# Six tiles of normalised rows transposed on VectorE, GpSimd and ScalarE instead of TensorE, and one product of the last network moved ahead of another

## The chip, the cores and the metric

The kernel runs on one core of one Trainium2 chip. The metric is the device time of one execution in microseconds (us). Three executions of the kernel before took 541.15, 541.38 and 541.42 us, the median being 541.38. A further execution was profiled; all rows below are from that one.

## The reference

Three stages follow each other. Attention with a local window and block summaries gives rows `x`; a network of eight experts with one expert per row gives new rows `x`; the last stage mixes them by a two-dimensional Fourier transform, normalises each row, and runs a dense network with 2048 hidden units. The change lies in the last stage only:

```python
def _moe2_ref(x, w_ch1, w_ch2):
    X = np.fft.fft(x, axis=1)
    X = np.fft.fft(X, axis=2)
    mixed = np.real(X).astype(np.float32)
    u = x + mixed
    mu = np.mean(u, axis=-1, keepdims=True)
    var = np.mean((u - mu) ** 2, axis=-1, keepdims=True)
    un = (u - mu) / np.sqrt(var + 1e-06)
    ch = np.maximum(un @ w_ch1, 0.0) @ w_ch2
    return (u + ch).astype(np.float32)
```

`x` has 2 x 768 rows of 512 numbers.

## The kernel before

The 1536 rows are twelve tiles of 128 rows, tile 0 to tile 11, and three chunks of four tiles: chunk 0 is tiles 0 to 3, chunk 1 tiles 4 to 7, chunk 2 tiles 8 to 11. The network's matmuls need a chunk's normalised rows with the 512 features on the partitions, so each tile is transposed. Every number is kept as a sum of a high and a low part (`h` and `l`, `fp32r`), and a product is three matmuls: high by high, high by low, low by high.

For one tile the steps are these. `ln_apply(i)` (L800 to L806) writes the normalised rows into a buffer `un` on ScalarE. `ln_T(i)` (L807 to L812) transposes its four 128x128 blocks on TensorE into a PSUM tile `lpt` (L810), ScalarE copies that into the high part `unh` of the chunk and VectorE writes the difference into the low part `unl` (L812). The buffers `un` come from a pool of four.

The network runs over 16 blocks of 128 hidden units, f = 0 to 15. `L1(c,f)` is 12 matmuls of 512 columns for chunk c into a PSUM tile `fph`; then `relu` writes the hidden units' high part `fhh` on ScalarE (L964) and their low part `fhl` on VectorE (L965). `L2(c,f)` is 12 matmuls from these into four PSUM tiles `fpy` (L985). `second()` issues the `L2` of the block before, so the order on TensorE is L1(f), L2(f-1), L1(f+1), L2(f), and so on. Chunk 0 runs all 16 blocks in the first loop (L1001). In it, beside the blocks f = 12 to 15, tiles 4 to 8 are normalised and tiles 4 to 7 transposed. Then comes a loop of eight blocks (L1073), numbered n = 0 to 7: L1(1,0) to L1(1,3) and L1(2,0) to L1(2,3). Beside n = 0 and n = 1 the tiles 8 to 11 are transposed. L1(1,0) reads all of chunk 1, that is tiles 4 to 7; L1(2,0) reads chunk 2.

The other 24 blocks of chunks 1 and 2 run in pairs (`pair`, L1047) by Strassen's scheme: seven half-size products `prod`, each 6 matmuls (L1052), are combined on VectorE into the first layer's results for two blocks and two chunks. `tt` (L1023) is VectorE's or GpSimd's addition. Three `ph` buffers in PSUM take the products in turn. The first pair has a part `begin` (L1093) in which VectorE and ScalarE still prepare factors of the products, `XT[0]` among them.

All engines execute in the order in which the code records their instructions; nothing reorders them. An engine that waits at one instruction holds back all that is recorded behind it.

Of the kernel before, what the change touches and what calls it, by code (L numbers as in the profile page):

```python
# [11 lines left out]
F32=mybir.dt.float32; R=mybir.dt.float32r; BF=mybir.dt.bfloat16; FH=mybir.dt.float16; I32=mybir.dt.int32; U8=mybir.dt.uint8  # L12
# [747 lines left out]
def fft_ffn(tc,ctx,fctx,tctx,cctx,plctx,I,ident,x2_dram,out,W,P,raw):  # L760
# [37 lines left out]
    def un_chunk(c,pool):  # L798
        UN[c]=tuple(pool.tile([128,4,512],R,name=f"un{x}{c}",tag=f"un{x}") for x in "hl")
    LP={}; TP=[None,None]  # L800
    def ln_apply(i,eng=None):
        un=LP.get(i) or unA.tile([128,512],F32,name=f"un{i}",tag="un",bufs=4)
        if i>3: S.activation(un,utile(i),AF.Identity,bias=nt[:,i:i+1],scale=rstd[:,i:i+1])
        elif eng is None: S.activation(un,utile(i),AF.Identity,bias=nb[:,i:i+1])
        else: eng.tensor_scalar(out=un,in0=utile(i),scalar1=nb[:,i:i+1],scalar2=None,op0=ALU.add)
        LP[i]=un  # L806
    def ln_T(i):  # L807
        un=LP.pop(i); c,q=divmod(i,4)
        pt=TP[0].tile([128,4,128],F32,name=f"lpt{i}",tag=TP[1])
# [152 lines left out]
    def hid(c,f): return [hp.tile([128,512],R,name=f"fh{n}{c}_{f}",tag="h"+n) for n in "hl"]  # L962
    def relu(h,x,o=slice(0,512)):
        S.activation(h[0][:,o],x,AF.Relu)  # L964
        V.scalar_tensor_tensor(out=h[1][:,o],in0=x,scalar=0.0,in1=h[0][:,o].bitcast(F32),op0=ALU.max,op1=ALU.subtract)  # L965
    def L1(c,f):
        g,k=divmod(f,4); h,l=W[g,0]; uh,ul=UN[c]
        ph=php.tile([128,512],F32,name=f"fph{c}_{f}",tag="ph"); n=0
        o=slice(128*k,128*k+128)
        for kd in range(4):  # L970
            for a,x in ((h,uh),(h,ul),(l,uh)):
                T.matmul(ph,lhsT=a[:,kd,o],rhs=x[:,kd],start=n==0,stop=n==11); n+=1  # L972
        H[c,f]=hid(c,f); relu(H[c,f],ph)
    def L2(c,f):
        g,k=divmod(f,4); wh,wl=W[g,1]; hh,hl=H.pop((c,f))
        if (c,f) in OPEN: PY[c]=[pyp.tile([128,512],F32,name=f"fpy{c}_{f}_{t}",tag=f"py{t}") for t in range(4)]
        for t in range(4):
            q=slice(128*t,128*t+128)
            if t==3 and c==2 and f>13:
                if f==15: PY[c][3]=(PY[c][3][:,0:256],ptp.tile([128,512],F32,name="fpy2_15_4",tag="pt")[:,0:256])  # L980
                outs=[(y,slice(256*n,256*n+256)) for n,y in enumerate(PY[c][3])]
            else: outs=[(PY[c][t],slice(0,512))]
            for y,o in outs:
                for i,(a,b) in enumerate(((hh,wh),(hh,wl),(hl,wh))):
                    T.matmul(y,lhsT=a[:,q],rhs=b[:,k,o],start=(c,f) in OPEN and i==0,stop=(c,f) in DONE and i==2)  # L985
                if (c,f)==(2,14): store(t,y,o)
    def fin(c,last,ts=range(4)):
        for t in ts:
            i=4*c+t; b,a,w=order[i]; u=utile(i)
            if c: tt(V,u,PY[c][t],u,ADD)  # L990
            else: V.scalar_tensor_tensor(out=u,in0=PY[c][t],scalar=rstd[:,i:i+1],in1=u,op0=ALU.mult,op1=ALU.add)
            o=b*768+w*384+a*128
            if last: nc.sync.dma_start(out[o:o+128],u)
# [3 lines left out]
    def second():  # L997
        if pend:
            c,f=pend.pop(0); L2(c,f)
            if (c,f) in DONE: fin(c,c==0)  # L1000
    for f in range(16):  # L1001
        if f==12: ln_apply(4)
        L1(0,f)
        for _ in range(1 if f in (2,4,7,10,12) else 2):
            if cv.busy: cv.step(); cv.load()
        if f<12: ln_stats((f+4)%12)
        if f==8: ln_rstd(slice(4,12))
        if f==12: ln_rstd(slice(0,4))
        if f==12:
            while cv.busy: cv.step(); cv.load()  # L1010
            rctx.close(); unB=ctx.enter_context(tc.tile_pool(name="unB",bufs=1)); un_chunk(1,unB)
        if f in (13,14): ln_T(2*f-22)
        if f in (13,14): ln_apply(2*f-21)
        if f==15: ln_apply(8)
        second(); pend.append((0,f))
        if f in (13,14):
            ln_T(2*f-21)
            if f==13: ln_apply(6)

    late=ctx.enter_context(tc.tile_pool(name="post",bufs=1)).tile([128,2,512],F32,name="post")  # L1020
# [23 lines left out]
    def pair(g,q,begin,ahead):  # L1044
        f=4*g+2*q; w=W[g,0]; n=[0]
        A=lambda i,j: [[a[:,2*j+k,256*q+128*i:256*q+128*i+128] for k in range(2)] for a in w]
        As=lambda s: [[a[:,s,256*q+128*k:256*q+128*k+128] for k in range(2)] for a in W[g-1,0]]  # L1047
        B=lambda j,k: [[a[:,2*j+i] for i in range(2)] for a in UN[k+1]]
        def prod(l,m):
            ps=php.tile([128,512],F32,name=f"fw{f}_{n[0]}",tag="ph"); n[0]+=1; i=0  # L1050
            for k in range(2):
                for a,b in ((0,0),(0,1),(1,0)): T.matmul(ps,lhsT=l[a][k],rhs=m[b][k],start=i==0,stop=i==5); i+=1  # L1052
            return ps
        def hidden(c,i,x): H[c,f+i]=hid(c,f+i); relu(H[c,f+i],x)
        S.copy(c12,prod(A(0,0),B(0,0))); tt(V,c11,prod(A(0,1),B(1,0)),c12,ADD)
        if begin: begin()
        split=ahead()
        tt(V,c12,prod(As(1),XT[1]),c12,ADD); hidden(1,0,c11)
        tt(V,c21,prod(As(2),XT[2]),c12,ADD)
        p=prod(As(0),XT[0]); tt(V,c22,p,c21,ADD); tt(V,c12,p,c12,ADD)  # L1060
        if begin: fin(2,False)
        tt(V,c21,prod(A(1,1),XT[3]),c21,ADD); hidden(1,1,c21)
        tt(V,c12,prod(As(3),B(1,1)),c12,ADD)
        if not begin: split()
        L2(1,f); hidden(2,1,c22); L2(1,f+1); fin(1,f==14); hidden(2,0,c12)
        if begin: split()
        L2(2,f+1); L2(2,f)
        if f<14: fin(2,False)
# [2 lines left out]
    D=[two(x) for x in xs]; pt=lambda: ptp.tile([128,512],F32,name="stage",tag="pt")  # L1071
    
    for n,(c,f) in enumerate([(1,0),(1,1),(1,2),(1,3),(2,0),(2,1),(2,2),(2,3)]):  # L1073
        if n==0: ln_apply(9)
        if n==2:
            t4=four(D+[None],X4,V,False); BG+=[x for y in t4[0:3] for x in y]
            un4=[unA.tile([128,512],R,name=f"xt{i}",tag="un",bufs=4) for i in range(4)]
            def last(k):
                p=pt(); h,l=X4(1,0); tt(V,p,h[:,k],D[1][:,k],SUB); tt(V,p,p,l[:,k],ADD); parts(un4[k],un4[2+k],p)
            BG+=[lambda k=k: last(k) for k in range(2)]  # L1080
            XT[3]=[un4[0:2],un4[2:4]]
        if n==6:
            sp=[pt()]; sp=[sp[0][:,256*(s%2):256*(s%2)+256] for s in range(4)]; z=weights(1,0,sp,V)
            for s in range(4): BG+=z[s]+[lambda s=s: parts(*place(1,0,s),sp[s])]
        if n==7:
            XT[1]=[[w[:,k] for k in range(2)] for w in W[0,1]]; parts(*[w[:,0:2] for w in W[0,1]],D[1])
        bg((0,0,3,3,2,2,4,6)[n])
        L1(c,f)
        if n<2: ln_T(8+2*n)
        if n==0: ln_apply(10); ln_apply(11)  # L1090
        second(); pend.append((c,f))
        if n<2: ln_T(9+2*n)
    def begin():  # L1093
        XT[2]=[[x[:,k] for k in range(2)] for x in UN[2]]; parts(*[x[:,0:2] for x in UN[2]],D[2])
        bg(4)
        c,f=pend.pop(0); L2(c,f)
        XT[0]=[[w[:,2+k] for k in range(2)] for w in W[0,1]]; parts(*[w[:,2:4] for w in W[0,1]],D[0])
        bg(99)
# [71 lines left out]
```

## Time and profile before

| | |
|---|---|
| median of 3 runs | 541.38 us |
| profiled execution | 541.06 us, of which span 539.2 us |
| TensorE matmuls busy | 526.5 us, 98% of the span |
| VectorE busy | 382.7 us, 71% |
| ScalarE busy | 276.6 us, 51% |
| GpSimd busy | 117.1 us, 22% |

The span runs from the first to the last instruction of the profile; the 1.9 us around it belong to the execution. PE is TensorE's matmuls, PEld its weight loads, DVE is VectorE, ACT ScalarE, POOL GpSimd. A name after L is a line of the kernel before. The modelled end of a matmul overlaps the next one, so the distance of two starts, not the duration, is what a matmul costs TensorE.

### The profile page before, as it was taken

How to read it: one execution, taken by the hardware profiler on the slowest of the kernel's cores; microseconds unless marked ns; L12 is line 12 of the kernel's file. 1: busy time of each engine (PE TensorE's matmuls, PEld its weight loads, DVE VectorE, ACT ScalarE, POOL GpSimd, SP SyncE). 2: the span in 40 equal slices, each digit the busy share in tenths (PEclk: the TensorE clock that was granted, in tenths of full speed). 3: DMA queues.
4: the chain of work that ended last, by engine and by line, in shares of the span. 5: the costliest groups of instructions: out<-in, count | busy, mean ns of one | idle time of the engine just before them, and what ended most of it. 6: DMA issues, size and time to landing. Idle time of an engine off the chain costs nothing.

```text
span 539.2 us, 9090 instructions
## 1 busy us (share of the span) xinstructions
PE 526.5 (98%) x3434; PEld 435.8 (81%) x3435; DVE 382.7 (71%) x731; ACT 276.6 (51%) x547; POOL 117.1 (22%) x163
## 2 busy tenths in 40 slices
PE   8999999999999999999999999999999999999996
PEld 4777778899999998887788888888887788888885
DVE  5778748797878887576887777516866866665664
ACT  5777775465776777543568987533023221221210
POOL 3225260302243202020540000000004345416000
PEclk9999999999999999999999999999999999999999
DMA  8999464698889886133045554002000000000004
GB/s 288 407 365 396 143 215 176 204 331 303 324 313 390 291 325 231 38 121 136 3 156 157 168 157 145 1 0 79 0 1 0 1 0 2 0 1 0 1 0 156
DMA packets 22735, 81.24 MB, mean 151 GB/s; under 512 B 2816, under 2 KB 4735, under 8 KB 19105
## 3 DMA queue, kind: packets, MB, share of 16 engines
q1 hardware_dynamic: 19249, 70.02, 36.6%
q0 software_dynamic: 3296, 10.48, 5.6%
q8 instruction: 28, 0.46, 0.3%
q14 instruction: 18, 0.15, 0.1%
q10 hardware_dynamic: 144, 0.13, 0.1%
HBM read 70.40 MB, written 9.96 MB: 149 GB/s over the span
## 4 chain that ended last, share of the span: by engine, by line
PE 53%; issue 3%; DVE 1%; ACT 0%; POOL 0%; DVEq 0%; POOLq 0%
PE fpy L985 24%; PE fph L972 12%; PE fw L1052 10%; PE py L582 1%; PE s1q L853 1%; PE lpt L810 1%; PE ph L565 1%; PE s L853 1%; PE pp L853 1%; PE big L582 1%; PE pq L853 1%; DVE dwr L1023 0%; DVE fwl L1023 0%; ACT fwh L1034 0%; PE s L867 0%
## 5 line engine op out<-in xcount | busy, mean ns | idle before, releaser
L985 PE MATMUL fpy<-fwh,fhh 128*128 128x512 f32 (+1 forms) x194 | 75.9, 391 | 0.0
L985 PE MATMUL fpy<-fwh,fhl 128*128 128x512 f32 (+1 forms) x194 | 75.5, 389 | 0.0
L985 PE MATMUL fpy<-fwl,fhh 128*128 128x512 f32 (+1 forms) x194 | 75.3, 388 | 0.0
L565 PE MATMUL ph<-xx,wh 128*128 128x256 f32 (+1 forms) x352 | 69.6, 290 | 1.6 <-DVEq L659 1.2
L552 DVE TENSOR_TENSOR wl<-wr,wh 128x1024 fp32r<-128x1024 f32 x46 | 54.6, 1222 | 13.6 <-ACT wh L551 13.5
L565 PEld LDWEIGHTS ph<-xx,wh 128*128 128x128 f32 x352 | 56.0, 191 | 3.7 <-ACTq L659 1.6
L551 ACT CAST wh<-wr 128x1024 fp32r<-128x1024 f32 (+1 forms) x50 | 48.3, 1014 | 12.6 <-PE py L582 7.1
L565 PE MATMUL ph<-xx,wl 128*128 128x256 f32 (+1 forms) x192 | 54.6, 292 | 0.0
L1023 POOL TENSOR_TENSOR dwr<-fwh 128x256 f32<-128x256 f32 x10 | 7.9, 788 | 173.5 <-DVE unl L1023 135.0
L1023 DVE TENSOR_TENSOR dwr<-fpy,dwr 128x512 f32<-128x512 f32 (+1 forms) x57 | 36.2, 676 | 10.5 <-PE fpy L985 10.5
L985 PEld LDWEIGHTS fpy<-fwh,fhl 128*128 128x128 f32 x194 | 36.4, 188 | 8.2 <-DVE fhl L965 0.4
L985 PEld LDWEIGHTS fpy<-fwh,fhh 128*128 128x128 f32 x194 | 36.5, 188 | 7.9 <-ACT fhh L964 0.4
L985 PEld LDWEIGHTS fpy<-fwl,fhh 128*128 128x128 f32 x194 | 36.5, 188 | 7.6
L972 PE MATMUL fph<-unh,fwh 128*128 128x512 f32 x96 | 38.1, 397 | 0.0
L972 PE MATMUL fph<-unh,fwl 128*128 128x512 f32 x96 | 37.7, 393 | 0.0
L972 PE MATMUL fph<-unl,fwh 128*128 128x512 f32 x96 | 37.7, 392 | 0.0
L582 PE MATMUL py<-wh,hh 128*128 128x512 f32 x92 | 36.8, 400 | 0.0
L565 PEld LDWEIGHTS ph<-xx,wl 128*128 128x128 f32 x192 | 36.1, 190 | 0.0
L582 PE MATMUL py<-wl,hh 128*128 128x512 f32 x92 | 36.1, 392 | 0.0
L582 PE MATMUL py<-wh,hl 128*128 128x512 f32 x92 | 36.0, 392 | 0.0
L589 POOL DMA_INDIRECT x_dram<-y,sidx x13 | 14.5, 1117 | 80.4 <-ACT y L587 48.0
L733 DVE SCALAR_TENSOR_TENSOR ft<-ft,fr 128x512 int32<-128x512 int32 x32 | 22.1, 691 | 12.6 <-ACT ft L732 12.5
(373 smaller groups left out, 1175.5 us busy)
## 6 DMA issues: line engine op xcount, KB each, us to landing
wr<-in_wm SPq DMA_DIRECT2D x24, 1024.0 KB, 7.6
fr<-in_wc SPq DMA_DIRECT2D x32, 512.0 KB, 3.6
kw<-in_kw SPq DMA_DIRECT2D x6, 720.0 KB, 11.1
vw<-in_vw SPq DMA_DIRECT2D x4, 1040.0 KB, 8.7
ft<-in_ft POOLq DMA_DIRECT2D x8, 436.0 KB, 9.5
x_dram<-xt SPq DMA_DIRECT2D x12, 256.0 KB, 5.5
dwr<-x_dram SPq DMA_DIRECT2D x12, 256.0 KB, 4.9
out<-dwr SPq DMA_DIRECT2D x11, 256.0 KB, 2.2
```

Of the source, the lines that this page charges most:

```text
L551: if 'h' in what: S.copy(wh[:,o],raw[:,o])
L552: if 'l' in what: eng.tensor_tensor(out=wl[:,o],in0=raw[:,o],in1=wh[:,o].bitcast(F32),op=ALU.subtract)
L565: T.matmul(ph,lhsT=a[:,o],rhs=b[:,kd],start=n==0,stop=n==11); n+=1
L582: T.matmul(PY[s][tt],lhsT=a[:,q],rhs=b[:,o],start=(c==0 and fb==0 and i==0),stop=(c==3 and fb==1 and i==2))
L589: st=G.indirect_dma_start(out=x2_dram[0:1152] if s==LAST else x2_dram,out_offset=IndirectOffsetOnAxis(ap=col,axis=0),in_=y,in_offset=None)
L733: V.scalar_tensor_tensor(out=ti,in0=ti,scalar=3,in1=low,op0=ALU.logical_shift_left,op1=ALU.bitwise_or)
L810: for kd in range(4): T.transpose(pt[:,kd],un[:,kd*128:kd*128+128],ident)
L853: T.matmul(ps,lhsT=ls[l],rhs=rs[r],start=first and n==0,stop=last and n==2); n+=1
L972: T.matmul(ph,lhsT=a[:,kd,o],rhs=x[:,kd],start=n==0,stop=n==11); n+=1
L985: T.matmul(y,lhsT=a[:,q],rhs=b[:,k,o],start=(c,f) in OPEN and i==0,stop=(c,f) in DONE and i==2)
L1023: def tt(e,o,x,y,op): e.tensor_tensor(out=o,in0=x,in1=y,op=op)
L1052: for a,b in ((0,0),(0,1),(1,0)): T.matmul(ps,lhsT=l[a][k],rhs=m[b][k],start=i==0,stop=i==5); i+=1
```

## The change

For tiles 4 to 9, `ln_T` is replaced by two new functions. `ln_S` has VectorE transpose each 32x32 block of the 128x512 tile within its place, from `un` into a buffer `tb`; 16 copies of 32 partitions x 4 x 32 numbers then move the blocks to their places in a buffer `xt_`, 10 of them on GpSimd (`G`) and 6 on ScalarE (`S`). `ln_P` then splits `xt_` into `unh` and `unl`; its operands lie in SBUF where those of L812 lay in PSUM. `un`, `tb` and `xt_` share the pool of four buffers. Tiles 10 and 11 keep `ln_T`. A table `plan`, read by `ln_at`, says before or after which block each step is recorded. It has ten entries, of which two stand below; A is `ln_apply`, B `ln_S`, C `ln_P`.

In the pair with `begin`, the product of `A(1,1)` and `XT[3]` is recorded before that of `As(0)` and `XT[0]`. Its use on VectorE stays in its place.

```diff
+    XS={}
+    def ln_S(i):
+        un=LP.pop(i)
+        b=unA.tile([128,512],F32,name=f"tb{i}",tag="un",bufs=4); XS[i]=unA.tile([128,512],F32,name=f"xt_{i}",tag="un",bufs=4).rearrange("p (k t) -> p k t",k=4)
+        V.transpose(b,un); b=b.rearrange("p (k j t) -> p k j t",k=4,j=4)
+        for q in range(4):
+            for j in range(4): (S.copy if (4*q+j)%8 in (2,5,7) else G.tensor_copy)(XS[i][32*j:32*j+32,:,32*q:32*q+32],b[32*q:32*q+32,:,j])
+    def ln_P(i):
+        x=XS.pop(i); c,q=divmod(i,4); o=slice(128*q,128*q+128); h,l=UN[c]
+        S.copy(h[:,:,o],x); V.tensor_tensor(out=l[:,:,o],in0=x,in1=h[:,:,o].bitcast(F32),op=ALU.subtract)
...
+    A,B,C=ln_apply,ln_S,ln_P
+    plan={(12,0):((A,4),),(12,1):((B,4),(A,5),(B,5)),(13,1):((C,4),(A,6),(B,6)),(13,2):((C,5),(A,7)),(14,1):((B,7),(C,6),(A,8)),
...
+    def ln_at(f,i):
+        for x,y in plan.get((f,i),()): x(y)
...
-        if f in (13,14): ln_T(2*f-22)
-        if f in (13,14): ln_apply(2*f-21)
-        if f==15: ln_apply(8)
+        ln_at(f,1)
...
         tt(V,c21,prod(As(2),XT[2]),c12,ADD)
+        if begin: p3=prod(A(1,1),XT[3])
         p=prod(As(0),XT[0]); tt(V,c22,p,c21,ADD); tt(V,c12,p,c12,ADD)
         if begin: fin(2,False)
-        tt(V,c21,prod(A(1,1),XT[3]),c21,ADD); hidden(1,1,c21)
+        tt(V,c21,p3 if begin else prod(A(1,1),XT[3]),c21,ADD); hidden(1,1,c21)
```

On ScalarE, from the last square root of the statistics to the activation of L1(0,14), the order before is this; `fph0_13` is L1's result for chunk 0 and block 13, and `lpt4` tile 4 transposed by TensorE:

```order
L783 ACTIVATE rstd_3493<-var_3492,eps_3498 128x4
L964 ACTIVATE fhh0_13_4650<-fph0_13_4637 128x512
L812 CAST unh1_4623<-lpt4_4654 128x4x128
L803 ACTIVATE un5_4661<-dwr1_3259,nt_3494,rstd_3493 128x512
L812 CAST unh1_4623<-lpt5_4675 128x4x128
L803 ACTIVATE un6_4682<-dwr1_3259,nt_3494,rstd_3493 128x512
L964 ACTIVATE fhh0_14_4697<-fph0_14_4684 128x512
```

The same stretch of ScalarE now, with `tb4` tile 4 transposed by blocks and `xt_4` tile 4 put together:

```order
L783 ACTIVATE rstd_3493<-var_3492,eps_3498 128x4
L819 COPY xt_4_4626<-tb4_4625 32x4x32 x6
L803 ACTIVATE un5_4644<-dwr1_3259,nt_3494,rstd_3493 128x512
L819 COPY xt_5_4647<-tb5_4646 32x4x32 x6
L974 ACTIVATE fhh0_13_4690<-fph0_13_4677 128x512
L822 CAST unh1_4623<-xt_4_4626 128x4x128
L803 ACTIVATE un6_4696<-dwr1_3259,nt_3494,rstd_3493 128x512
L819 COPY xt_6_4699<-tb6_4698 32x4x32 x6
L822 CAST unh1_4623<-xt_5_4647 128x4x128
L803 ACTIVATE un7_4731<-dwr1_3259,nt_3494,rstd_3493 128x512
L974 ACTIVATE fhh0_14_4746<-fph0_14_4733 128x512
```

Twelve copies and one `un` now stand ahead of the activation of block 13, and six more copies with two casts and two `un` ahead of that of block 14.

On VectorE, behind the last step of the statistics, the order before is this (`fhl0_13` is the low part of block 13's hidden units):

```order
L789 TENSOR_TENSOR nt_3494<-nb_3495,rstd_3493 128x4
L965 SCALAR_TENSOR_TENSOR fhl0_13_4651<-fph0_13_4637,fhh0_13_4650 128x512
L812 TENSOR_TENSOR unl1_4624<-lpt4_4654,unh1_4623 128x4x128
L812 TENSOR_TENSOR unl1_4624<-lpt5_4675,unh1_4623 128x4x128
L965 SCALAR_TENSOR_TENSOR fhl0_14_4698<-fph0_14_4684,fhh0_14_4697 128x512
L812 TENSOR_TENSOR unl1_4624<-lpt6_4701,unh1_4623 128x4x128
L812 TENSOR_TENSOR unl1_4624<-lpt7_4722,unh1_4623 128x4x128
L965 SCALAR_TENSOR_TENSOR fhl0_15_4743<-fph0_15_4729,fhh0_15_4742 128x512
```

And now:

```order
L789 TENSOR_TENSOR nt_3494<-nb_3495,rstd_3493 128x4
L817 STREAM_TRANSPOSE tb4_4625<-un4_4590 128x512
L817 STREAM_TRANSPOSE tb5_4646<-un5_4644 128x512
L975 SCALAR_TENSOR_TENSOR fhl0_13_4691<-fph0_13_4677,fhh0_13_4690 128x512
L822 TENSOR_TENSOR unl1_4624<-xt_4_4626,unh1_4623 128x4x128
L817 STREAM_TRANSPOSE tb6_4698<-un6_4696 128x512
L822 TENSOR_TENSOR unl1_4624<-xt_5_4647,unh1_4623 128x4x128
L975 SCALAR_TENSOR_TENSOR fhl0_14_4747<-fph0_14_4733,fhh0_14_4746 128x512
L817 STREAM_TRANSPOSE tb7_4750<-un7_4731 128x512
L822 TENSOR_TENSOR unl1_4624<-xt_6_4699,unh1_4623 128x4x128
L975 SCALAR_TENSOR_TENSOR fhl0_15_4799<-fph0_15_4785,fhh0_15_4798 128x512
L822 TENSOR_TENSOR unl1_4624<-xt_7_4751,unh1_4623 128x4x128
```

The transposition of tile 7 now stands behind `fhl0_14`, and the low part of tile 7 behind `fhl0_15`.

On TensorE, in the first pair, the products 4 and 5 stood so; `fwh0_1` and `fwl0_1` are the two parts of `XT[0]`, `xt0` to `xt3` those of `XT[3]`:

```order
L1052 MATMUL fw4_4_5157<-fwh0_1_2206,fwh0_0_2204 128x512
L1052 MATMUL fw4_4_5157<-fwl0_1_2207,fwh0_0_2204 128x512
L1052 MATMUL fw4_4_5157<-fwh0_1_2206,fwl0_0_2205 128x512
L1052 MATMUL fw4_4_5157<-fwh0_1_2206,fwh0_0_2204 128x512
L1052 MATMUL fw4_4_5157<-fwl0_1_2207,fwh0_0_2204 128x512
L1052 MATMUL fw4_4_5157<-fwh0_1_2206,fwl0_0_2205 128x512
L1052 MATMUL fw4_5_5170<-xt0_4870,fwh1_0_2208 128x512
```

and now:

```order
L1063 MATMUL fw4_4_5241<-xt0_4954,fwh1_0_2208 128x512
L1063 MATMUL fw4_4_5241<-xt2_4956,fwh1_0_2208 128x512
L1063 MATMUL fw4_4_5241<-xt0_4954,fwl1_0_2209 128x512
L1063 MATMUL fw4_4_5241<-xt1_4955,fwh1_0_2208 128x512
L1063 MATMUL fw4_4_5241<-xt3_4957,fwh1_0_2208 128x512
L1063 MATMUL fw4_4_5241<-xt1_4955,fwl1_0_2209 128x512
L1063 MATMUL fw4_5_5248<-fwh0_1_2206,fwh0_0_2204 128x512
```

The two products have changed places; the other orders of the pair are as before.

## Rows read from the trace of the kernel before

**Rows 1.** Page, part 1: busy time, share of the span, instructions by engine.

```profile
PE 526.5 (98%) x3434; PEld 435.8 (81%) x3435; DVE 382.7 (71%) x731; ACT 276.6 (51%) x547; POOL 117.1 (22%) x163
```

**Rows 2.** Windows: us, busy (instructions) by engine, TensorE clock, DMA share, GB/s.

```profile
345.00:360.00 15.00, 15.00 (x75) 12.39 (x74) 4.65 (x7) 7.07 (x12) 0.00 (x0) 1.00 0.00 0
```

**Rows 3.** Timeline around tile 4's transposition: start, duration, engine, line, operation, [idle <-releaser].

```profile
344.40 0.16 DVE L789 TENSOR_TENSOR nt<-nb,rstd 128x4 f32<-128x4 f32 x1
...
345.15 0.40 PE L972 MATMUL fph<-unh,fwl 128*128 128x512 f32 x1
...
345.38 0.60 PE L810 MATMUL lpt<-ident,un 128*128 128x128 f32 x4
345.58 0.60 ACT L964 ACTIVATE fhh<-fph 128x512 fp32r<-128x512 f32 x1 [2.22 <-PE fph L972]
...
346.06 0.39 PE L985 MATMUL fpy<-fwl,fhh 128*128 128x512 f32 x1
...
346.22 0.69 DVE L965 SCALAR_TENSOR_TENSOR fhl<-fph,fhh 128x512 fp32r<-128x512 f32 x1 [1.65 <-ACT fhh L964]
```

**Rows 4.** Timeline where L1(1,0) begins.

```profile
358.90 1.51 ACT L803 ACTIVATE un<-dwr,nt,rstd 128x512 f32<-128x512 f32 x2
...
360.93 0.40 PE L972 MATMUL fph<-unh,fwh 128*128 128x512 f32 x1
...
361.17 0.40 PE L972 MATMUL fph<-unl,fwh 128*128 128x512 f32 x1
```

**Rows 5.** Lines by form, ACT: xcount | busy us, mean ns | idle before.

```profile
L738 ACT CAST fwh<-ft 128x512 fp32r<-128x512 f32 x32 | 19.5, 610 | 1.5 <-DVE ft L734 1.2 <-ACT ft L732 0.3
L964 ACT ACTIVATE fhh<-fph 128x512 fp32r<-128x512 f32 x24 | 14.2, 590 | 27.0 <-PE fph L972 27.0
L803 ACT ACTIVATE un<-dwr,nt,rstd 128x512 f32<-128x512 f32 x8 | 6.3, 814 | 0.0
L841 ACT CAST Qd<-xe 128x255 fp32r<-128x255 f32 x3 | 1.2, 402 | 3.2 <-DVE xe L840 3.2
L922 ACT ACTIVATE Qd<-ident 128x3 fp32r<-128x3 f32 x2 | 0.3, 195 | 0.0
```

**Rows 6.** Timeline of ACT in the attention: four activations in a row.

```profile
63.15 1.12 ACT L166 ACTIVATE a<-sc,nm 128x120 f32<-128x120 f32 x4
```

**Rows 7.** Lines by form, DVE.

```profile
L965 DVE SCALAR_TENSOR_TENSOR fhl<-fph,fhh 128x512 fp32r<-128x512 f32 x24 | 16.5, 689 | 20.1 <-ACT fhh L964 20.1
L1023 DVE TENSOR_TENSOR dwr<-dwr,unl 128x1024 f32<-128x1024 f32 x4 | 4.9, 1222 | 0.1
L805 DVE TENSOR_SCALAR un<-dwr,nb 128x512 f32<-128x512 f32 x1 | 0.6, 591 | 0.0
```

**Rows 8.** Lines by form, POOL.

```profile
L119 POOL COPY kw<-ks 128x288 f32<-128x288 f32 x6 | 2.6, 434 | 7.4 <-DVE ks L118 7.4
L124 POOL COPY kw<-k 128x384 f32<-128x384 f32 x2 | 1.1, 556 | 0.0
```

**Rows 9.** Timeline of POOL in the Fourier stage.

```profile
266.27 0.63 POOL L907 TENSOR_TENSOR dwr<-dwr,ch 128x255 f32<-128x255 f32 x1
266.87 1.96 POOL L906 TENSOR_TENSOR dwr<-dwr,ch 128x257 f32<-128x257 f32 x1
```

**Rows 10.** Timeline of the first pair, from product 4 on.

```profile
415.54 0.40 PE L1052 MATMUL fw<-fwh,fwh 128*128 128x512 f32 x1
...
416.51 0.50 PE L1052 MATMUL fw<-fwl,fwh 128*128 128x512 f32 x1 [0.57 <-DVE fwl L1023]
...
417.53 0.39 PE L1052 MATMUL fw<-fwh,fwl 128*128 128x512 f32 x1
...
418.36 0.69 DVE L1023 TENSOR_TENSOR dwr<-fw,dwr 128x512 f32<-128x512 f32 x1
...
423.41 0.19 PEld L985 LDWEIGHTS fpy<-fwh,fhh 128*128 128x128 f32 x1 [0.37 <-ACT fhh L964]
...
424.14 0.19 PEld L985 LDWEIGHTS fpy<-fwh,fhl 128*128 128x128 f32 x1 [0.43 <-DVE fhl L965]
```

More of the change, by code (lines that the diff above doesn't have):

```diff
@@ L1000, in second @@
             if (c,f) in DONE: fin(c,c==0)
+    A,B,C=ln_apply,ln_S,ln_P
+    plan={(12,0):((A,4),),(12,1):((B,4),(A,5),(B,5)),(13,1):((C,4),(A,6),(B,6)),(13,2):((C,5),(A,7)),(14,1):((B,7),(C,6),(A,8)),
+          (15,1):((C,7),(B,8),(A,9)),(16,1):((C,8),(B,9),(A,10)),(16,2):((A,11),),(17,1):((C,9),(ln_T,10)),(17,2):((ln_T,11),)}
+    def ln_at(f,i):
+        for x,y in plan.get((f,i),()): x(y)
     for f in range(16):
-        if f==12: ln_apply(4)
+        ln_at(f,0)
         L1(0,f)
@@ L1011, in fft_ffn @@
             rctx.close(); unB=ctx.enter_context(tc.tile_pool(name="unB",bufs=1)); un_chunk(1,unB)
-        if f in (13,14): ln_T(2*f-22)
-        if f in (13,14): ln_apply(2*f-21)
-        if f==15: ln_apply(8)
+        ln_at(f,1)
         second(); pend.append((0,f))
-        if f in (13,14):
-            ln_T(2*f-21)
-            if f==13: ln_apply(6)
+        ln_at(f,2)
     late=ctx.enter_context(tc.tile_pool(name="post",bufs=1)).tile([128,2,512],F32,name="post")
@@ L1073, in fft_ffn @@
     for n,(c,f) in enumerate([(1,0),(1,1),(1,2),(1,3),(2,0),(2,1),(2,2),(2,3)]):
-        if n==0: ln_apply(9)
         if n==2:
@@ L1087, in fft_ffn @@
         bg((0,0,3,3,2,2,4,6)[n])
[L1088 to L1092, printed above, removed]
+        L1(c,f); ln_at(16+n,1)
+        second(); pend.append((c,f)); ln_at(16+n,2)
     def begin():
```

## The prediction

> **What bounds the kernel now.** Read the page's first part first: TensorE's matmuls are busy for 98% of the span [rows 1], so time leaves the kernel only where TensorE loses work or a wait, and comes in only where it meets a new wait. Then read the stretch of the change by windows: from 345 to 360 us TensorE is busy throughout, ScalarE for 7.07 of 15 us, VectorE for 4.65, GpSimd not at all [rows 2]. These three have room for more work, but a share says nothing of the order in which it must end. So read the timeline last, and look for the two moments that have a deadline: where L1(1,0) begins, which needs all of tiles 4 to 7 [rows 4], and where the first pair waits [rows 10].
>
> **What goes from TensorE.** The last product before tile 4 starts at 345.15, the four transpositions follow at 345.38, which is the ordinary distance of 0.23, and the second product of the next block stands at 346.06 [rows 3]. Without the transpositions that would be two distances, 0.46; it is 0.91. So one tile costs TensorE 0.45 us. Six tiles go: 6 x 0.45 = 2.7 us, if nothing new is waited for.
>
> **What comes, and its prices.** Per tile, VectorE gets one 32x32-block transposition of 128x512, ScalarE six copies of 128 numbers per partition, GpSimd ten. The trace has none of the three.
> - Transposition: a VectorE instruction over 128x512 takes 0.59 (one input) to 0.69 (two), over 128x1024 1.22 [rows 7]. I take 0.68, and keep 0.59 and 1.22 as ends. The Trainium skill (VectorE: DVE Perf Modes, "The three transpose paths") gives VectorE 311 ns for a 128x128 bf16 transposition; four of these would be an estimate of 1.24, and the sum would end 2.2 us higher.
> - ScalarE's copy: 3 numbers take 0.195 and 255 take 0.402 [rows 5], so 128 some 0.30. Two activations of 0.814 each were done in 1.51 [rows 4, 5], so the next starts 0.1 before the end of the one in front: 0.20 per copy, 1.20 for six. Ends: 0.10 (the 3-number row less the overlap) and 0.28 (four of 120 in 1.12 [rows 6]).
> - GpSimd's copy: 288 numbers took 0.434, 384 took 0.556 [rows 8]; on that line 128 take 0.23. I take 0.25, so 2.5 per tile, with ends 0.23 and 0.43 (no cheaper than 288).
> - A handover from engine to engine costs 0.04 to 0.05 (the activation of 345.58 ends at 346.18, its VectorE follower starts at 346.22); from TensorE it is 0.43 after the start of the last product (345.15 to 345.58) [rows 3].
>
> **The chain to tile 7.** Before, the tiles waited for TensorE. Now the recorded order makes one chain through ScalarE and VectorE, since the copies of tile 5 stand ahead of block 13's activation, those of tile 6 behind it, and tile 7's transposition behind block 14's low part. It starts when the statistics are done, at 344.40 + 0.16 = 344.56 [rows 3]. With activation 0.59, cast 0.63 (a little over the 0.61 of the nearest row), `un` 0.82 [rows 5] and the 0.1 of overlap:
> 1. tile 4: handover, transposition 0.68, handover, six copies 1.20: 346.54.
> 2. tile 5: `un` 0.82, transposition 0.73, copies 1.25: 349.34.
> 3. activation of block 13 0.49, cast of tile 4 0.53, `un` 6 0.82, transposition 0.73, copies 1.25: 353.16.
> 4. cast of tile 5 0.53, `un` 7 0.72, activation of block 14 0.59, its low part on VectorE 0.66, transposition of tile 7 0.68, copies 1.25: 357.59.
> 5. cast of tile 6 0.53, `un` 8 0.72, activation of block 15 0.49, cast of tile 7: 359.96. VectorE's low part of block 15 ends in turn at 360.09, that of tile 7 at 360.78; handover: 360.83.
>
> L1(1,0)'s second product, the first to need a low part, started at 361.17 [rows 4]. With four tiles' transpositions gone, TensorE would be there at 361.17 - 4 x 0.45 = 359.37. So it will wait about 1.4 us in front of L1(1,0) and start its second product 0.34 earlier than before. Block 13's and 14's hidden units still come in time: the low parts are ready at 350.7 and 355.7, and TensorE, at 12 products of 0.23 per block from 345.38 on, wants them at about 351.4 and 356.9.
>
> Behind it, tiles 8 and 9 no longer cost TensorE anything: 2 x 0.45 = 0.9. Chunk 2 is wanted three blocks later, and tiles 10 and 11 find ScalarE in time. Sum of this part: -0.34 - 0.9 = -1.25 us.
>
> The buffers add one wait: the copies of tile 5 write where `tb` of tile 4 lay, so ScalarE's copies, and behind them block 13's activation, wait for GpSimd's ten of tile 4. At 0.25 those end at 347.9, before tile 5's transposition (348.09): no cost. The casts likewise wait for GpSimd's copies. If GpSimd's copy takes p, the chain by GpSimd alone puts tile 7's low part at about 348.5 + 40p; it passes the 360.83 from p = 0.31 on. That is the number that matters most here.
>
> A rule speaks against the change. In the Fourier stage GpSimd's addition, 0.63 us beside it, took 1.96 while VectorE read two SBUF inputs [rows 9]. The Trainium skill (GPSIMD Engine Reference, "Key points") says that GpSimd shares its SBUF interfaces with VectorE, with contention where VectorE has two SBUF inputs. The trace agrees with it; `unl` from `xt_` and `unh` is such an instruction now. If each held GpSimd for its 0.69, p would be 0.32 in effect, the sum -0.7 instead of -1.25. In the chain above the low parts fall mostly behind GpSimd's copies, so I leave it at nothing.
>
> **The product moved ahead.** TensorE stood still before product 4's second matmul (416.51, 0.57 idle, for `XT[0]`'s low part) [rows 10]. The moved product's six matmuls fill that gap, so TensorE gets ahead by about 0.84 (from 415.54 to 416.51 where 0.23 is due, and 0.1 behind it). But what is late next is VectorE. Product 4 now ends later: its last matmul starts at 415.54 + 11 x 0.23 = 418.07 instead of 417.53. VectorE's sum from it began at 418.36, and could begin 0.43 after that start, at 418.50: 0.15 later, with rounding. From there VectorE goes on in order through the four `fin` additions to the moved product's sum, block 5's activation and its low part, and for these TensorE already waits (423.41, 0.37 idle for `fhh`; 424.14, 0.43 for `fhl`). So TensorE's lead of 0.84 is spent in that wait and the end comes 0.15 later.
>
> **Sum.** 541.06 (span 539.2 and what lies around it) - 1.25 + 0.15 = 540.0 for the profiled execution. The median of the runs, 541.38, lies 0.3 above it; between 540.0 and 540.3 I say 540.2. What a measurement of this kernel tells from no change is 0.2%, 1.1 us; the forecast sits at that edge.
>
> The bounds: all 24 ScalarE copies of the chain at 0.10 would take 2.4 off it, at 0.28 put 1.9 on; the four transpositions at 0.59 take 0.4 off, at 1.22 put 2.2 on. The gain cannot exceed the 2.7 of TensorE (and 0.84): 537.5. GpSimd at 0.43 gives 348.5 + 17.2 = 365.7, so +4.5 - 0.9, and about 1.5 of waits of the same kind at tiles 10 and 11: 546.3.
>
> **Rivals.**
> - All of it is hidden: the copies are cheap enough that tile 7 is there by 359.4. For it: ScalarE's shortest rows and its idle 2.22 before block 13's activation [rows 3]. Against: the chain would have to lose 1.4 of 16.3 us. Then -2.7 + 0.15: 538.5.
> - The moved product pays its 0.84, VectorE having slack I don't see: 540.0 - 0.15 - 0.84 = 539.0. Against it stand the two waits for `fhh` and `fhl`.
> - Slower: GpSimd's copies are dear. A 32-partition copy with two strides costs 0.40 rather than 0.25, the ten copies of each tile hold ScalarE through the shared buffers, and block 13's and 14's activations and L1(1,0) come late. From p = 0.335 on the gain is gone (348.5 + 40p = 361.17 + 0.9 - 0.15). At 0.40: 364.5, +3.3 - 0.9 + 1.2 of later waits + 0.15, 544.8. For it: GpSimd's rows vary, and none has this shape.
> - No difference: the transposition takes about 1.0, or ScalarE's copies 0.25; then tile 7 is 1.2 later and the sum is near zero, 541.3.
>
> **How the numbers follow.** Forecast (the ScalarE chain ends 0.3 before the old start): 0.42, own range 539.3 to 541.2, half of it below 540.3, which is 0.2% under the median. All hidden 0.15; the moved product pays 0.08; GpSimd dear 0.22; no difference 0.13. Faster: 0.21 + 0.15 + 0.08 = 0.44. Same: 0.21 + 0.13 = 0.34. Slower: 0.22. The range takes in the hidden case and the lower half of the dear one: 538.3 to 543.6.
>
> **What would show it.** Right: a wait of 1 to 2 us on TensorE in front of L1(1,0), released by VectorE's `unl`; six ScalarE copies in about 1.2; ten GpSimd copies in 2.5 or less; no wait at block 13's and 14's second layer; in the first pair no gap at product 4, and one of over 1 us in front of block 5's second layer. Wrong: ScalarE waiting for GpSimd ahead of tile 5's copies; a transposition well off 0.7 us; no wait at L1(1,0).

## The result, and the profile after

| | median us (lowest to highest) | ratio to before, 95% interval | profiled execution: us, span, clock |
|---|---|---|---|
| before | 541.26 (540.95 to 541.42) | 1 | 541.06, 539.2, 0.999 |
| after | 545.95 (545.05 to 546.61) | 1.0085 (1.007 to 1.0101) | 545.05, 542.9, 0.995 |
| after, run again beside the experiments | 545.07 (544.19 to 545.78) | 1.0064 (1.0051 to 1.0078) | 544.58, 542.4, 1.0 |

The change makes the kernel 0.6 to 0.9% slower; 540.2 was forecast, and 545.95 is above the range's end of 543.6 too. Each ratio, here and below, is to executions of the kernel before that were made beside it; their median was 541.26 for the first and 541.78 to 542.41 for the others. TensorE's busy time reads 526.5 us as before [rows 1], although the 24 transpositions of six tiles are gone from it, so the saving does not show in that number; the span grew by 3.7 (page, first part, of after; busy us, share of the span, instructions):

```profile
span 542.9 us, 9151 instructions
PE 526.5 (97%) x3411; PEld 434.1 (80%) x3411; DVE 386.4 (71%) x737; ACT 287.2 (53%) x583; POOL 136.1 (25%) x223
```

**Where L1(1,0) begins.** TensorE's rows of after (start, duration, engine, line, operation, idle time before and what ended it), for [rows 4]:

```profile
359.96 0.40 PE L995 MATMUL fpy<-fwh,fhl 128*128 128x512 f32 x1
362.80 0.49 PE L982 MATMUL fph<-unh,fwh 128*128 128x512 f32 x1 [2.44 <-ACT unh L822]
363.53 0.67 PE L982 MATMUL fph<-unl,fwh 128*128 128x512 f32 x1 [0.23 <-DVE unl L822]
363.99 0.63 PE L982 MATMUL fph<-unh,fwl 128*128 128x512 f32 x1
364.42 0.63 PE L982 MATMUL fph<-unh,fwh 128*128 128x512 f32 x1
```

The foreseen wait is there and ends with the foreseen instructions, but the second product starts at 363.53, not at 360.83, and 2.36 later than before. The next ones stand 0.43 apart in place of 0.23: the clock has halved. Windows of after (two), then of its second run (length, busy time of PE, PEld, DVE, ACT, POOL, then the granted clock):

```profile
365.00:366.00 1.00, 1.00 (x4) 0.81 (x3) 0.00 (x0) 0.96 (x4) 0.88 (x4) 0.50 0.00 0
363.00:368.00 5.00, 4.77 (x14) 3.54 (x14) 1.09 (x2) 2.65 (x8) 2.88 (x10) 0.66 0.00 0
```
```profile
363.00:368.00 5.00, 4.62 (x19) 3.55 (x20) 1.72 (x4) 3.33 (x10) 2.86 (x10) 1.00 0.00 0
```

A smaller wait that was not foreseen stands at block 13's second layer:

```profile
351.16 0.50 PE L995 MATMUL fpy<-fwh,fhh 128*128 128x512 f32 x1 [0.24 <-ACT fhh L974]
```

**What came late.** ScalarE, VectorE and GpSimd of after, from tile 4's transposition to tile 7's low part:

```profile
344.42 0.70 DVE L817 STREAM_TRANSPOSE tb<-un 128x512 f32<-128x512 f32 x1
345.16 1.84 ACT L819 COPY xt<-tb 32x128 f32<-32x128 f32 x6 [1.85 <-DVE tb L817]
345.28 3.25 POOL L819 COPY xt<-tb 32x128 f32<-32x128 f32 x10 [68.21 <-DVE tb L817]
347.01 0.82 ACT L803 ACTIVATE un<-dwr,nt,rstd 128x512 f32<-128x512 f32 x1
...
348.70 3.25 POOL L819 COPY xt<-tb 32x128 f32<-32x128 f32 x10 [0.17 <-DVE tb L817]
...
350.51 0.60 ACT L974 ACTIVATE fhh<-fph 128x512 fp32r<-128x512 f32 x1
...
353.31 1.83 ACT L819 COPY xt<-tb 32x128 f32<-32x128 f32 x6 [0.83 <-DVE tb L817]
353.34 3.66 POOL L819 COPY xt<-tb 32x128 f32<-32x128 f32 x10 [1.38 <-DVE tb L817]
355.16 0.62 ACT L822 CAST unh<-xt 128x512 fp32r<-128x512 f32 x1
...
355.82 0.69 DVE L822 TENSOR_TENSOR unl<-xt,unh 128x512 fp32r<-128x512 f32 x1 [2.54 <-ACT unh L822]
...
358.41 1.83 ACT L819 COPY xt<-tb 32x128 f32<-32x128 f32 x6 [1.43 <-DVE tb L817]
358.46 3.64 POOL L819 COPY xt<-tb 32x128 f32<-32x128 f32 x10 [1.46 <-DVE tb L817]
360.27 0.62 ACT L822 CAST unh<-xt 128x512 fp32r<-128x512 f32 x1
...
362.13 0.62 ACT L822 CAST unh<-xt 128x512 fp32r<-128x512 f32 x1
362.78 0.69 DVE L822 TENSOR_TENSOR unl<-xt,unh 128x512 fp32r<-128x512 f32 x1
```

Six ScalarE copies in a row take 1.83 to 1.84, so 0.305 each; 1.20 was assumed. In these rows ScalarE waits for nothing but VectorE's transpositions, and its copies of tiles 4 to 7 end at 347.0, 350.5, 355.1 and 360.2, where 346.54, 349.34, 353.16 and 357.59 were forecast. GpSimd's copies of tile 7 end at 362.10, and ScalarE's last cast starts at 362.13. So close together, the two engines leave open which of them sets the time; e5 to e7 decide it. The groups by form (count, busy us, mean ns):

```profile
L819 ACT COPY xt<-tb 32x128 f32<-32x128 f32 x36 | 10.6, 296 | 8.2 <-DVE tb L817 7.9
L819 POOL COPY xt<-tb 32x128 f32<-32x128 f32 x60 | 18.1, 301 | 78.8 <-DVE tb L817 76.5
L817 DVE STREAM_TRANSPOSE tb<-un 128x512 f32<-128x512 f32 x6 | 4.2, 706 | 2.7 <-ACT un L803 2.7
```

**The first pair** of after, for [rows 10] (product 4 is `As(0)` by `XT[0]`, as there; it starts at 420.40):

```profile
419.57 0.68 DVE L1034 TENSOR_TENSOR post<-fw,post 128x512 f32<-128x512 f32 x1
419.85 0.40 PE L1063 MATMUL fw<-xt,fwl 128*128 128x512 f32 x1
420.40 0.47 PE L1063 MATMUL fw<-fwh,fwh 128*128 128x512 f32 x1
422.06 0.69 DVE L1034 TENSOR_TENSOR dwr<-fw,dwr 128x512 f32<-128x512 f32 x1 [0.61 <-PE fw L1063]
424.10 0.47 PE L995 MATMUL fpy<-fwh,fhh 128*128 128x512 f32 x1 [0.69 <-DVE dwr L1034]
427.12 0.19 PEld L995 LDWEIGHTS fpy<-fwh,fhh 128*128 128x128 f32 x1 [0.48 <-ACT fhh L974]
427.84 0.19 PEld L995 LDWEIGHTS fpy<-fwh,fhl 128*128 128x128 f32 x1 [0.43 <-DVE fhl L975]
```

The 0.57 gap within product 4 is gone, but product 4 itself starts 0.32 late (420.40; due 0.23 after 419.85): it now gets the PSUM buffer that VectorE reads from 419.57 to 420.25. VectorE's sum from it starts later still, at 422.06. TensorE's lead is used up by a new wait at 424.10 (0.69, in front of block 4's second layer, for VectorE's sums that read the `fpy` buffers), and the waits for `fhh` and `fhl` behind it are about as long as before (0.48 for 0.37, 0.43 for 0.43).

### The profile page after: what moved, and what is told of

Same layout as the page of the kernel before. It is cut to its first block, busy times and chain, and to the rows that moved or that the text cites. A ratio compares the mean times of both kernels' runs of the same rounds, so it can differ in the third digit from the quotient of the medians.

```text
span 542.9 us, 9151 instructions
## 1 busy us (share of the span) xinstructions
PE 526.5 (97%) x3411; PEld 434.1 (80%) x3411; DVE 386.4 (71%) x737; ACT 287.2 (53%) x583; POOL 136.1 (25%) x223
## 4 chain that ended last, share of the span: by engine, by line
PE 47%; DVE 4%; ACT 3%; issue 3%; POOL 0%; DVEq 0%; ACTq 0%; POOLq 0%
PE fpy L995 20%; PE fph L982 11%; PE fw L1063 10%; ACT xt L819 1%; DVE dwr L1034 1%; PE py L582 1%; PE s1q L863 1%; PE ph L565 1%; PE s L863 1%; ACT fhh L974 1%; ACT un L803 1%; PE pp L863 1%; DVE tb L817 1%; PE lpt L810 1%; PE big L582 1%
## 5 line engine op out<-in xcount | busy, mean ns | idle before, releaser
L819 POOL COPY xt<-tb 32x128 f32<-32x128 f32 x60 | 18.1, 301 | 78.8 <-DVE tb L817 76.5
```

The source lines that it names most:

```text
L819: for j in range(4): (S.copy if (4*q+j)%8 in (2,5,7) else G.tensor_copy)(XS[i][32*j:32*j+32,:,32*q:32*q+32],b[32*q:32*q+32,:,j])
```

## The experiments

Three distances are read from TensorE's rows of each profile: D1 from block 13's first product to L1(1,0)'s second; D2 from the same to the first of L1(1,3); P from the first pair's third product (`As(1)` by `XT[1]`) to the weight load that waits for `fhl`. Clock: granted in L1(1,0). e5 to e7 ran once each, so only the distances inside their profiles are used. A blank is a distance on which the run has no bearing.

| kernel | D1 | D2 | P | clock | median us | ratio (95%) |
|---|---|---|---|---|---|---|
| before | 18.51 | 36.72 | 11.36 | full | | 1 |
| after | 20.93 | 39.93 | 11.91 | half | 545.95 | 1.0085 |
| after_again | 20.94 | 38.98 | 11.90 | full | 545.07 | 1.0064 |
| e1 | 20.93 | 38.95 | 11.43 | full | 544.11 | 1.0047 (1.0034 to 1.006) |
| e2 | | | 11.87 | | 542.0 | 1.0009 (0.9995 to 1.0023) |
| e3 | | | 11.51 | | 541.87 | 1.0004 (0.9977 to 1.0031) |
| e4 | 20.95 | 38.98 | | full | 545.19 | 1.0066 (1.0048 to 1.0083) |
| e5 | 23.06 | | | half | 548.65, one run | |
| e6 | 20.02 | 39.45 | | half | 544.13, one run | |
| e7 | 20.88 | 39.89 | | half | 544.95, one run | |
| e8 | | 39.00 | | full | 544.16 | 1.0026 (1.0001 to 1.0052) |
| e9 | 16.57 | 37.45 | | full | 541.8 | 0.9996 (0.9969 to 1.0023) |
| e10 | 16.56 | 33.05 | | full | 540.4 | 0.9973 (0.9958 to 0.9987) |
| e11 | 16.56 | 34.79 | | full | 540.86 | 0.9985 (0.9965 to 1.0005) |

**e1: after, with the product put back.**
```diff
-        if begin: p3=prod(A(1,1),XT[3])
-        tt(V,c21,p3 if begin else prod(A(1,1),XT[3]),c21,ADD)
+        tt(V,c21,prod(A(1,1),XT[3]),c21,ADD)
```


> The changed kernel, with the product on the last weights block put back behind the fourth product. Theory: moving the product costs 0.56 us (the way from VectorE's c11 to the first weight load that waits for fhl took 13.70 us after and 13.14 before), so this kernel is 0.56 faster than the changed one: 545.4 where that one has 545.95. Rival (the prediction's term): 0.15 faster. Rival: the moved product gave back its 0.84, so this one is 0.8 slower, 546.8. In every case the rest of the loss (some 4 us) stays, as it lies in the network's tiles.


P falls from 11.91 to 11.43, 0.48 of the 0.55 that it had grown; D1 stays at 20.93. So the loss has two separate parts, and the larger one lies in the tiles.

**e2: before, with the product ahead alone; e3: the same in a bank of its own** (shortened: e3 also lets `prod` take the bank).
```diff
+        if begin: p3=prod(A(1,1),XT[3])         # e3: prod(A(1,1),XT[3],pt())
-        tt(V,c21,prod(A(1,1),XT[3]),c21,ADD)
+        tt(V,c21,p3 if begin else prod(A(1,1),XT[3]),c21,ADD)
```


> The kernel before, with the product on the last weights block ahead as the only change. Theory: 0.56 slower than before, 541.8, with a wait of 0.3 us in front of the fourth product for the PSUM buffer that VectorE is still reading. Rival (the prediction's term): 0.15 slower, 541.4. Rival: 0.84 faster, 540.4.

> The kernel before, with the product ahead, but accumulated in a PSUM bank of its own, so that the fourth product keeps the buffer that came free early. Theory: the 0.3 us wait in front of the fourth product goes, and with it most of the cost: 0.15 to 0.25 over the kernel before, 541.4 to 541.5, and 0.3 to 0.4 under the kernel with the product alone. Rival: the buffer is not the cause, and VectorE is late by itself: as slow as the kernel with the product alone.


In the profiles P grows by 0.51 in e2 and by 0.15 in e3: the buffer is the cause of the difference, and 0.15 is left, the term of the prediction. The times are level with before within their intervals and don't separate the two; the rows do. Around product 4, e2, then e3:

```profile
417.55 0.40 PE L1052 MATMUL fw<-xt,fwl 128*128 128x512 f32 x1
418.05 0.47 PE L1052 MATMUL fw<-fwh,fwh 128*128 128x512 f32 x1
```
```profile
417.03 0.39 PE L1052 MATMUL stage<-xt,fwl 128*128 128x512 f32 x1
417.25 0.39 PE L1052 MATMUL fw<-fwh,fwh 128*128 128x512 f32 x1
```

**e4: after, with ten products whose result nobody reads.**
```diff
+        if n==0:
+            z=pt()
+            for k in range(10): T.matmul(z,lhsT=W[0,0][0][:,k%4,0:128],rhs=UN[0][0][:,k%4],start=k==0,stop=k==9)
         L1(c,f); ln_at(16+n,1)
```


> The changed kernel, with ten extra products (2.3 us of work, written to a PSUM bank that nobody reads) in TensorE's queue in front of L1(1,0), where it stood still for 2.8 us. Theory: the clock fell because TensorE stood still; with the wait filled, the ten products of L1(1,0) that took 0.43 us take 0.23, and the kernel is 1.6 to 1.7 us faster than the changed one, 544.3, with the second product of L1(1,0) at the same 363.5. Rival: those products are slow for another reason (their operands, just written by ScalarE and VectorE, or the copies running beside them): no gain, 545.9.


The products of L1(1,0) took 0.23, yet D2 fell by 0.95, not by 1.6: TensorE then runs into a wait for tile 10's activation on ScalarE. And e1, with no filling, kept its clock too. So e4 does not show that the filling did it.

**after_again: after, unchanged.**


> The changed kernel once more, unchanged, for what is open about the clock: in the one profile of it the clock fell to half behind the wait in front of L1(1,0), in the same kernel with the product order of before, and the same wait, it did not. Theory: it falls in some executions and not in others, since nothing in the kernel differs; then this profile shows either ten products of 0.43 or of 0.23 in L1(1,0), the wait of tile 10 for ScalarE appears only where the clock held, and the spans of the runs spread by 1 us or more. Rival: the moved product, or something else in the program, makes the difference: the clock falls again, with the same 3.2 us at L1(1,3).


The same program, the same stretch of standing still, and this time the full clock. TensorE then meets tile 10:

```profile
372.57 0.66 PE L810 MATMUL lpt<-ident,un 128*128 128x128 f32 x4 [0.29 <-ACT un L803]
```

D2 is 38.98 as in e1 and e4. In its six timed executions two had a mean clock of 1.0 and spans of 542.0 and 542.4, four had 0.995 to 0.997 and spans of 542.8 to 543.6: about 1.0 us, if a mean clock under 1.0 stands for the same fall; where those four fell is not on record. The moved product is not its cause: the clock held here with it, and fell in e5 to e7 without it.

**e5: each ScalarE copy in two halves of the same partitions** (shortened; e5 to e7 have e1's product order).
```diff
-                    S.copy(x,y)
+                    S.copy(x[:,0:2],y[:,0:2])
+                    S.copy(x[:,2:4],y[:,2:4])
```


> The changed kernel with the product order of before (so that only the tiles differ); each of ScalarE's six copies per tile is two copies of half the numbers, with the same start partitions. What is read is the distance from the first product of block 13's first layer to the second product of L1(1,0), 20.93 us in the changed kernel and 18.51 before. Theory: ScalarE's copies sit in the chain to tile 7 and no copy overlaps the one in front of it; 12 copies of about 0.245 us (between 0.195 for 3 numbers and 0.297 for 128) take 2.95 a tile in place of 1.83, so L1(1,0) is 4 x 1.1 = 4.5 us later, distance 25.4. Second theory: the overlap of 0.1 that the longer activations show is lost only where the start partitions change; then 2.4 a tile and a distance of 23.2, and the two halves of a pair start 0.15 apart. Rival: ScalarE's copies are not in the chain (GpSimd's are): distance 20.9 to 21.5.


The second theory holds. L822 is a first half, L823 the second:

```profile
346.89 0.24 ACT L822 COPY xt<-tb 32x64 f32<-32x64 f32 x1 [1.85 <-DVE tb L817]
347.04 0.24 ACT L823 COPY xt<-tb 32x64 f32<-32x64 f32 x1
347.29 0.25 ACT L822 COPY xt<-tb 32x64 f32<-32x64 f32 x1
347.44 0.24 ACT L823 COPY xt<-tb 32x64 f32<-32x64 f32 x1
```

A second half starts 0.15 after the first, 0.09 before that ends; the next pair, on other partitions, starts 0.25 after, when it has ended. And of the 4 x 0.57 = 2.3 us that this adds for four tiles, 2.13 show up in D1: the copies are in the chain.

**e6: ScalarE's copies on VectorE; e7: GpSimd eight, VectorE two.**
```diff
-(S.copy if (4*q+j)%8 in (2,5,7) else G.tensor_copy)
+(V.tensor_copy if (4*q+j)%8 in (2,5,7) else G.tensor_copy)                                            # e6
+(S.copy if (4*q+j)%8 in (2,5,7) else V.tensor_copy if (4*q+j)%8==4 else G.tensor_copy)                # e7
```


> The changed kernel with the product order of before; the six copies per tile that ScalarE made are made by VectorE. Theory: ScalarE's chain is what came late, and GpSimd stands close behind it: ten copies of 3.3 to 3.65, then 0.7 for the next transposition, four times in turn from 345.28 on, then cast and low part, put the second product of L1(1,0) at 362.2, a distance of 19.6 in place of 20.93. Rival: GpSimd binds already: 20.9. Rival: VectorE's copies hold GpSimd's up, as both use SBUF: over 21.

> The changed kernel with the product order of before; GpSimd makes eight copies a tile in place of ten, VectorE makes the other two, ScalarE its six as before. Theory: ScalarE's chain binds and GpSimd ends just before it: 0.3 us gained at most, distance 20.6 to 20.9. Rival (GpSimd's copies are the price that decides, as the prediction's slower rival had it): 4 x 2 x 0.33 = 2.6 us gained, distance 18.3.


Fewer GpSimd copies (e7) give 0.05: in the changed kernel ScalarE binds. No ScalarE copies (e6) give 0.9 (1.3 expected), and the cast of tile 7 then waits for GpSimd. Tile 7 in e6:

```profile
357.85 3.61 POOL L819 COPY xt<-tb 32x128 f32<-32x128 f32 x10 [0.88 <-DVE tb L817]
361.49 0.62 ACT L822 CAST unh<-xt 128x512 fp32r<-128x512 f32 x1 [2.37 <-POOL xt L819]
```

**e8 and e9: tiles started early.** Both have e1's product order and send tiles 8 to 11 the new way as well; how they share out the copies stands in their expectations, and the diff shows the plans alone.
```diff
+plan={(10,1):((A,4),(B,4)),(11,1):((A,5),(B,5)),(12,1):((C,4),(C,5),(A,6),(B,6)),(13,1):((A,7),(B,7)),(13,2):((C,6),),...   # e8
+plan={(10,1):((A,4),(B,4)),(12,0):((A,5),(B,5)),(13,1):((C,4),(A,6),(B,6)),(13,2):((C,5),(A,7)),(14,1):((B,7),(C,6)),(14,2):((C,7),),
+      (15,1):((A,8),(B,8),(A,9),(B,9)),(16,1):((C,8),(C,9),(A,10),(B,10)),...                                               # e9
```


> A version meant to beat both: product order as before; tiles 4 and 5 are prepared behind blocks 10 and 11, with all 16 copies on GpSimd, which is idle there; tiles 6 and 7 follow at blocks 12 and 13; tiles 8 to 11 all go by VectorE's transposition and the copies too, from block 14 on. Theory: nothing about the new operations is dear when they stand outside a chain with a deadline; no wait is left in front of L1(1,0), tile 7's low part is there by 355, and TensorE saves 8 x 0.45 = 3.6 us: 3.6 under the kernel before, 538.2 against 541.8, ratio 0.9934. Rival: contention on SBUF between GpSimd, VectorE and ScalarE slows the work of the blocks around it, and half or more of the gain is lost: 540 or above.

> The second version meant to beat both, after the first lost 3.8 us at block 13's second layer and some 2 more to the half clock behind it. Product order as before; only tile 4 is prepared early (behind block 10, all copies on GpSimd), tile 5's transposition stands ahead of the statistics of chunk 0, from tile 5 on GpSimd makes 8 copies, ScalarE 6 and VectorE 2, and the cast of tile 7 stands ahead of block 15's activation; tiles 8 to 11 as in the first version. Theory: ScalarE's chain starts with tile 5 at 343 to 344 and is one tile shorter, so tile 7's low part is there at about 358.5 in the time of before, TensorE does not stand still at L1(1,0) and keeps its clock, and all 8 x 0.45 = 3.6 us are gained: ratio 0.9934. Rival: the copies of tile 4 slow VectorE's conversion of the weights beside them, tile 5 comes late again, and TensorE waits 1 us or more at block 13 or at L1(1,0): gain 2.6 or less.


Both lose their gain to a new wait: e8 at block 13's second layer, since GpSimd's 16 copies beside the weights' conversion were slow and tile 5, then block 13's activation, stood behind them (and the clock fell behind the wait: 0.66 in the mean from 355 to 360); e9, with L1(1,0) free at last (D1 16.57), at L1(1,0)'s own second layer, for `fin(0)`, which stood behind tile 10 on VectorE. (`fin(c)` is VectorE's four additions of chunk c's results in the `fpy` buffers to the rows; the next chunk's second layer writes the same buffers.) One row each, and GpSimd's 16 copies in e9 (0.51 each):

```profile
355.12 0.50 PE L995 MATMUL fpy<-fwh,fhh 128*128 128x512 f32 x1 [3.78 <-ACT fhh L974]
```
```profile
336.38 8.09 POOL L819 COPY xt<-tb 32x128 f32<-32x128 f32 x16 [58.51 <-DVE tb L817]
...
370.83 0.47 PE L995 MATMUL fpy<-fwh,fhh 128*128 128x512 f32 x1 [2.60 <-DVE dwr L1001]
```

**e10: all eight tiles, mended; e11: tiles 4 to 7 alone** (shortened).
```diff
+      (15,1):((A,8),(B,8)),(16,1):((A,9),(B,9)),(16,2):((C,8),(A,10),(B,10)),(17,1):((C,9),(A,11),(B,11)),(17,2):((C,10),),(18,1):((C,11),)}  # e10
-        bg((0,0,3,3,2,2,4,6)[n])          # e10: in front of L1 ...
         L1(c,f); ln_at(16+n,1)
+        bg((0,0,3,3,2,2,4,6)[n])          # ... and now behind it
+      (15,1):((A,8),),(15,2):((A,9),),(16,1):((ln_T,8),(A,10),(A,11)),(16,2):((ln_T,9),),(17,1):((ln_T,10),),(17,2):((ln_T,11),)}            # e11
```


> The last version with its new wait mended: tiles 4 to 7 stay as they are there (TensorE went through L1(1,0) without standing still); what cost it 2.6 us and the half clock was fin(0) on VectorE, which stood behind tile 10's transposition and the activations of tile 9's copies. Here tiles 8 to 11 go without ScalarE (12 copies on GpSimd, 4 on VectorE), tiles 10 and 11 stand behind fin(0), and VectorE's weight sums stand behind each block's low part in place of ahead of it. Theory: no wait of TensorE is left between 343 and 410, 8 x 0.45 = 3.6 us less than before: ratio 0.9934, 538.2 for 541.8. Rival: GpSimd's 12 copies (4.0 us a tile, more where VectorE reads two inputs) end tile 11 too late for L1(2,0), and a wait of 1 us or more stands there: gain under 2.6.

> The same with tiles 4 to 7 alone on the new way and tiles 8 to 11 transposed by TensorE as in the kernel before. Theory: 4 x 0.45 = 1.8 us less than before, with no wait at L1(1,0) and none behind it: ratio 0.9967. Rival: tile 8's to 11's work on ScalarE and VectorE is pushed back by the new copies and a wait comes behind block 16: gain under 1 us.


e10 beats both kernels: 0.27% under before, less than the 0.66% hoped for. Up to L1(1,3) the whole gain is there (36.72 - 33.05 = 3.67). Then TensorE waits for `fin(1)`, since VectorE is late: its weight sums stand behind tile 11's low part, that waits for ScalarE's cast, and the cast for GpSimd's twelve copies. From there on VectorE works without a pause up to `fin(1)`:

```profile
375.74 4.34 POOL L819 COPY xt<-tb 32x128 f32<-32x128 f32 x12 [0.81 <-DVE tb L817]
380.11 0.62 ACT L822 CAST unh<-xt 128x512 fp32r<-128x512 f32 x1 [4.03 <-POOL xt L819]
380.76 0.69 DVE L822 TENSOR_TENSOR unl<-xt,unh 128x512 fp32r<-128x512 f32 x1 [2.55 <-ACT unh L822]
...
389.75 2.47 DVE L1033 TENSOR_TENSOR dwr<-dwr,unl 128x1024 f32<-128x1024 f32 x2
392.14 2.48 DVE L1033 TENSOR_TENSOR dwr<-fpy,dwr 128x512 f32<-128x512 f32 x4
392.97 0.47 PE L995 MATMUL fpy<-fwh,fhh 128*128 128x512 f32 x1 [1.83 <-DVE dwr L1033]
```

By these rows the rival had the cause right, GpSimd's copies of tile 11, and the size (a gain under 2.6), but not the place: it had put the wait at L1(2,0). Behind the wait 1.3 of the 3.67 are left. That the profile's span, 539.1, is level with before's all the same comes from block 13, which began 1.09 later in it (343.75 for 342.66), ahead of the stretch looked at. e11 gains 1.93 up to L1(1,3) (36.72 - 34.79), and its span is 1.6 shorter (537.6 for 539.2; block 13 began 0.34 later in it); its time is 0.98 lower, and the interval just reaches 1, so its gain is shown by the profile alone. e10 with fewer copies on GpSimd, or with `fin(1)` ahead of the sums, was not tried.

## Why the prediction was wrong

- **TensorE's saving: right.** Four tiles less are 1.95 in e11's D1 (18.51 - 16.56), 0.49 each for the 0.45 assumed; eight are 3.67 in e10.
- **The chain to tile 7: right in its mechanism, wrong in two prices, and either alone was enough to turn the sign of D1.** First, ScalarE's copies: "so the next starts 0.1 before the end of the one in front: 0.20 per copy, 1.20 for six" took the overlap from two activations on the same 128 partitions [rows 4, 5]. Here each copy goes to other partitions, and e5 shows that the overlap is lost there. The duration, 0.30, was right; the pitch is 0.305, above even the bound of 0.28 [rows 6]. By the prediction's own sum this is 4 x (1.83 - 1.20) = 2.5 of the 2.7 us by which L1(1,0)'s second product missed 360.83, and e7 shows that it is the price that binds.
- **GpSimd: p is 0.33, not 0.25,** and 0.366 where VectorE reads two SBUF inputs beside it (3.66 for ten in tile 6, with `unl` at 355.82 in the middle, 3.25 in tile 4, with none). The Trainium skill (GPSIMD Engine Reference, "Key points") names that contention, and these rows agree; leaving it at nothing was wrong. Over tiles 4 to 7 the mean is 0.345, past the break-even of 0.335, so this rival would have come true without ScalarE's error too: with ScalarE's copies gone (e6), GpSimd alone keeps D1 1.51 over before. Putting ScalarE's price right would therefore have won back 0.9 us and no more. The formula was good: 348.5 + 40p gives 362.3, and e6 has 342.66 + 20.02 = 362.7 in the time of before.
- **Block 13's and 14's hidden units: late, where they were said to come in time.** Block 13's low part was ready at 351.8, not at 350.7, and TensorE waited there. The longer wait at L1(1,0) stands behind it, so this adds nothing of its own.
- **The transposition: right** (0.70 for 0.68); the estimate of 1.24, worked out from the Trainium skill (VectorE: DVE Perf Modes, "The three transpose paths"), is not borne out.
- **Tiles 8 and 9, -0.9: mostly not paid.** With the full clock D2 is 2.26 over before and D1 2.43, so 0.17 came of it: ScalarE, behind with everything, brings tile 10 late.
- **The moved product: right in sign, 0.55 for 0.15.** The term of 0.15 is what e3 shows; the rest is the PSUM buffer in turn, which the step left out. The lead is spent in front of block 4's second layer; the prediction had put that in front of block 5's.
- **The clock: not foreseen.** About 1.0 us (D2 of after less that of its second run: 0.95), in some executions.

Sum in the profiled execution of after: D2 3.21 + P 0.55 = 3.76; the span grew by 3.7.

## What to carry to other kernels

Moving work off the busiest engine pays only where what replaces it has a chain shorter than the time until it is wanted; a chain through an in-order engine pays every instruction on it, so a price per copy that is off by 0.1 us counts 24 times. Begun earlier and with the copies shared out otherwise, the replacement of four tiles kept all that TensorE saved up to the end of e11's profile. When two engines share such work, check what is left if only one of their prices is put right. Take the price of back-to-back instructions from rows that have the same change of partitions, not only the same size. When an operation is moved ahead in a loop with rotating PSUM buffers, look at which buffer each later one now gets, and who still reads it.

## What the runs showed of the hardware

ScalarE's overlap of successive copies (0.09 us) was there when the partitions stayed and absent when they changed (e5). TensorE's clock fell from 2.4 to 1.2 GHz for about 3 us behind a wait of 2.8 us in some executions of a program and not in others (granted clock 0.50 and 1.00 in the windows above); why it falls in one and not in the next stays open. GpSimd's copy of 32x128 took 0.33 with no two-input VectorE instruction beside it, 0.37 in the mean of ten with one such beside them, 0.51 beside the weights' conversion on VectorE (e9).
